# Mixing four chunks of attention logits with quarter-array products instead of four full-array products

## The chip, the cores and the metric

The kernel runs on one core of one Trainium2 chip. The metric is the device time of one execution in microseconds (us). The kernel before was timed three times: 578.25, 578.26 and 579.37 us, median 578.26 us.

## The reference, cut to what matters

Talking-heads attention over 8 batches, 12 heads, 448 positions and 64 dimensions, followed by a feed-forward layer:

```python
scores = scale * np.matmul(q, k.transpose(0, 1, 3, 2))          # per head
scores = np.einsum('bhij,hg->bgij', scores, w_pre)              # heads mixed before the softmax
attn = np.exp(scores - np.max(scores, axis=-1, keepdims=True))
attn = attn / (np.sum(attn, axis=-1, keepdims=True) + 1e-09)
attn = np.einsum('bhij,hg->bgij', attn, w_post)                 # heads mixed after the softmax
attn_out = np.matmul(attn, v)
x = attn_out.transpose(0, 2, 1, 3).reshape(8 * 448, 768)
h = np.maximum(x @ w_in, 0.0)                                   # 768 -> 2048
out = (h * h) @ w_out                                           # 2048 -> 768
```

## The kernel before

**Chunks.** The mixing of heads is a 12 by 12 matrix applied to the logits of one query position. The kernel handles ten query positions at a time: a *chunk* is 10 positions by 12 heads, so 120 partitions by 448 keys. A batch has 45 chunks, in four blocks: a short block of 6 (the last 64 positions), and three blocks of 13 chunks, of which the first of each (`cc == 0`) takes positions left over from two blocks and the other 12 are regular. There are 360 chunks in all.

**One chunk's way through the engines.** `score` (L681) makes the logits of one head for 128 query positions on TensorE. With 64 dimensions to contract, two heads use the two halves of the array's rows at the same time. VectorE (DVE) or ScalarE (ACT) copies each result from its PSUM bank to `snat` (L487 and L489 are the two branches of the helper `copy`, so all copies have these lines). `relayout` then issues a DMA on SP's queue, which gathers ten positions of all twelve heads from `snat` into one of eleven buffers `sch`. `chunk` then records, in this order:

- the mix on TensorE (L807): one product of the 120 x 128 weight `wmix` (ten copies of the 12 by 12 matrix on the diagonal) with `sch`, 448 columns into one PSUM bank;
- the minimum of each row on DVE (L818; the weights carry the sign and the scale, so the minimum stands for the maximum), and the exponential with its row sum on ACT (L821), which frees the bank;
- a reciprocal for two chunks at a time on DVE (L827), and on GpSimd (POOL) `wq` (L830), the second mixing matrix times the reciprocals;
- four products on TensorE that transpose and mix the attention weights (L837), and their copy to `atb` on DVE or ACT.

There are six buffers each of `es` (the exponentials) and `wq`. When a half batch is complete, `av` (L882) multiplies by `v`, two heads side by side in the two halves of the array's columns. Then units of the feed-forward layer follow: L941 is its first product, L955 or L959 the relu, L962 the square on POOL, L980 the second product, and L1004 the store. In batch 0, 14 chunks are made by another way (L813); the change leaves these alone.

**What sets the order.** Everything is recorded as an `Op` with a priority, dependencies and a guessed duration, and the class `Planner` simulates the engines once, at build time, and writes one fixed order for each engine. At run time each engine takes its list in that order and waits on semaphores. Feed-forward products have the lowest priority and fill what the attention leaves free. The planner hands out the eight PSUM banks; `MOST` bounds how many each kind of work may hold ("m" logits, "a" transposed weights, "f" feed-forward, "g" scores and `av`; "mix" all but "f"). It also knows a mode of the array for each product: `ROWS` for two row halves, `COLS` for two column halves, and it counts `TURN = 95` ns where the mode changes. `AHEAD` says how many chunks ahead of its use a gather is due. The products of `still` (L1191) are fillers without a result; the kernel has 44 of them in the early part of the run.

Of the kernel before, what the change touches and what calls it, by code (L numbers as in the profile page):

```python
# [23 lines left out]
NJ = 3  # L24
# [5 lines left out]
KC = CI * H  # L30
C0 = [0, 6, 19, 32]
# [9 lines left out]
NE = 6  # L41
NSCH = 11
AHEAD = 7.0
# [3 lines left out]
ROWS, COLS = 1, 2  # L47
# [5 lines left out]
STAY = {ROWS: 2, COLS: 6}  # L53
# [4 lines left out]
MOST = {"m": 3, "a": 2, "f": 2, "g": 6, "mix": 7}  # L58
# [245 lines left out]
def kernel(  # L304
# [30 lines left out]
    sch = many(NSCH, "sch", [KC, S], BF16)  # L335
    schl = sb.tile([KC, S], BF16, name="schl")
    es = many(NE, "es", [KC, S], BF16)
    mn = many(NE, "mn", [KC, 1], F32)
    sm = many(NE // 2, "sm", [KC, 2], F32)
    rc = many(NE // 2, "rc", [KC, 2], F32)  # L340
    wq = many(NE, "wq", [KC, H, CI], BF16)
# [49 lines left out]
    wpre_rep = sb.tile([KC, H], F32, name="wpre_rep")  # L391
    wpost_rep = sb.tile([KC, H], F32, name="wpost_rep")
    smask = sb.tile([KC, CI], F32, name="smask")
    wmix = many(3, "wmix", [KC, P], BF16)
    for t_ in wmix:
        nc.vector.memset(t_[:, KC:P], 0.0)
    wback = sb.tile([KC, H, CI], F32, name="wback")
    nmask = sb.tile([KC, CI], F32, name="nmask")
    perm = sb.tile([KC, KC], BF16, name="perm")

    own = sb.tile([KC, H], F32, name="own")
# [14 lines left out]
    def pick(to, of, mask):  # L416
        parts = hr[0][0:KC, 0:H * H].rearrange("p (g h) -> p g h", g=H)
        nc.vector.tensor_tensor(
            out=parts, in0=wall[0:KC, H * H * of:H * H * (of + 1)].rearrange("p (h g) -> p g h", g=H),
            in1=mask[:, :].unsqueeze(1).to_broadcast([KC, H, H]), op=ALU.mult,  # L420
        )
        nc.vector.tensor_reduce(out=to[:, :], in_=parts, axis=AX.X, op=ALU.add)

    def pick_near():
        nc.vector.tensor_reduce(
            out=own[:, :], in_=ident[0:KC, 0:KC].rearrange("p (s h) -> p h s", s=CI), axis=AX.X, op=ALU.add,
        )
        pick(wpre_rep, 0, own)
        pick(wpost_rep, 1, own)
# [23 lines left out]
    def near_masks():  # L453
        nc.vector.tensor_reduce(
            out=smask[:, :], in_=ident[0:KC, 0:KC].rearrange("p (s h) -> p s h", s=CI), axis=AX.X, op=ALU.add,
        )
        nc.vector.tensor_scalar(
            out=nmask[:, :], in0=smask[:, :], scalar1=-SCALE, scalar2=1.0, op0=ALU.mult, op1=ALU.mult,
        )
        nc.vector.tensor_copy(  # L460
            out=perm[:, :].rearrange("k (s x p) -> k s x p", s=CI, x=2),
            in_=ident[0:KC, 0:KC].rearrange("k (s p x) -> k s x p", s=CI, x=2),
        )

    def near_mix():
        for t_ in wmix[1:]:
            nc.vector.tensor_tensor(
                out=t_[:, 0:KC].rearrange("p (s h) -> p s h", s=CI),
                in0=wpre_rep[:, :].unsqueeze(1).to_broadcast([KC, CI, H]),
                in1=nmask[:, :].unsqueeze(2).to_broadcast([KC, CI, H]), op=ALU.mult,  # L470
            )

    def near_back():
        nc.gpsimd.tensor_tensor(
            out=wback[:, :, :], in0=wpost_rep[:, :].unsqueeze(2).to_broadcast([KC, H, CI]),
            in1=smask[:, :].unsqueeze(1).to_broadcast([KC, H, CI]), op=ALU.mult,
        )
# [237 lines left out]
    def relayout(b, c):  # L715
# [8 lines left out]
        if r == 2 and cc == 0:  # L724
            src_of[n] = schl
            here.append(move(n, pri, 780, deps + side.get(b - 1, []), schl[24:96, :], sn[120:126, :, :], lat))
            return
# [12 lines left out]
        else:  # L740
            parts = [(blk, 0, KC, sn[cc - 1:cc + CPR * (CI - 1):CPR, :, :])]
        for of, r0, r1, srcs in parts:
            ns = 860 if r1 - r0 > 90 else 590
            relay_of.setdefault(of, []).append(move(n, pri, ns, deps + old, src_of[n][r0:r1, :], srcs, lat))
        if r == 0 and cc == 5 and b > 0:
            here.append(move(
                place_of(b, C0[2]), pri + 0.5, 500, deps + side.get(b - 1, []),
                schl[0:24, :], sn[124:P, 0:NPAIR, :], lat,
# [17 lines left out]

    def chunk(b, c):
        n = place_of(b, c)
        r, cc = block_of(c)
        rows = 96 if c == C0[2 if b else NJ] else KC  # L770
        ns = rows // H
        far = is_direct(b, c)
        src = None if far else src_of[n]
        wm = wmix[0 if r == 0 else 2 if cc == 0 and r < NJ else 1]
        back = wback_far if far else wback
# [75 lines left out]
        m = m_op[n] = add(  # L851
# [13 lines left out]
        w = wq_op[n] = add("POOL", 370, n + 0.5, f_wq, [s_, at_op.get(n - NE)] + (backed_far if far else backed), lat=70)  # L865
# [147 lines left out]
    def pieces(pair, pos, part=None):  # L1013
        e0, e1 = (0, DMODEL) if part is None else part
        got = []
        for bb in range(2):
            row = (2 * pair + bb) * S
            for j, first in enumerate(PLACES[bb]):
# [9 lines left out]
                view = out[row:row + CPR * CI * NJ, :].rearrange("(s c r) e -> r c s e", c=CPR, r=NJ)  # L1028
# [24 lines left out]
    def w_turn(slot):  # L1053
        nc.tensor.matmul(
            slot[0:KC, 0:KC], lhsT=perm[:, :], rhs=wmix[1][:, 0:KC], start=True, stop=True,
        )

    def w_put():
        for t_, hi in ((wmix[0], KC), (wmix[2], 24)):
            nc.vector.tensor_copy(out=t_[0:hi, 0:KC], in_=slots["m", "w"][0:hi, 0:KC])  # L1060
# [6 lines left out]
    backed.append(add("POOL", 420, NEAR_AT, near_back, [fetched, masked]))  # L1067
# [78 lines left out]
    def next_batch(b):  # L1146
# [11 lines left out]
        for r in range(NJ + 1):  # L1158
            for p in groups(b, r):
                score(b, r, p)  # L1160
            for c in range(C0[r], (C0 + [NCHUNK])[r + 1]):
                relayout(b, c)
# [26 lines left out]
    def stand(slot, mode):  # L1189
        k_, m_ = P // 2 if mode == ROWS else P, P // 2 if mode == COLS else P  # L1190
# [41 lines left out]
```

## Time and profile before

| | |
|---|---|
| median of three runs | 578.26 us |
| profiled execution, its own time | 577.99 us |
| its span, first to last instruction | 576.2 us |
| granted TensorE clock, mean over the span | 0.999 |
| TensorE products (PE) busy | 565.1 us, 98% |
| VectorE (DVE) busy | 510.2 us, 89% |
| ScalarE (ACT) busy | 445.9 us, 77% |
| GpSimd (POOL) busy | 329.4 us, 57% |

In the page, busy time of an engine is the union of its instructions. A product's own duration holds its way through the array, so neighbours overlap: what one costs on a full engine is the distance between the starts of two neighbours, which the timeline shows. The profiled execution's time is 1.8 us more than its span.

### The profile page before, as it was taken

The page shows a single profiled execution, that of the slowest core. Times are in us where ns is not written, and L with a number is a line of the kernel's source. Part 1 is how long each engine was busy: PE and PEld are TensorE (multiplying, and loading weights), DVE is VectorE, ACT ScalarE, POOL GpSimd, SP SyncE. Part 2 cuts the span into 40 slices and gives each one's busy share as a digit, 9 for nine tenths or more (in the row PEclk, how much of TensorE's full clock was granted, in tenths as well). Part 3 has the DMA queues.
Part 4 walks back from the last instruction along what each step waited for, and adds up shares of the span by engine and source line. Part 5 has one row for each costly group of instructions (what it writes and reads, how often), then busy time and mean ns, then how long its engine had stood idle before and what let it go on. Part 6 is the DMA issues. An engine that isn't in the chain of part 4 may idle for free.

```text
span 576.2 us, 16829 instructions
## 1 busy us (share of the span) xinstructions
PE 565.1 (98%) x5830; PEld 407.5 (71%) x5830; DVE 510.2 (89%) x1124; ACT 445.9 (77%) x1185; POOL 329.4 (57%) x609
## 2 busy tenths in 40 slices
PE   8999999999999999999999999999999999999997
PEld 5668766786776767677667677777758676767784
DVE  7999998999999999989899988999799898989442
ACT  5798988878778887988888988888888888888100
POOL 8267445764575548646567357845767444735341
PEclk9999999999999999999999999999999999999999
DMA  9999849963898639963697638984497646322021
GB/s 135 211 182 224 158 116 208 163 151 87 132 202 156 159 100 184 173 151 111 137 181 148 164 104 144 188 152 139 109 205 158 147 121 117 124 81 75 1 56 55
DMA packets 131678, 80.79 MB, mean 140 GB/s; under 512 B 59286, under 2 KB 126600, under 8 KB 131592
## 3 DMA queue, kind: packets, MB, share of 16 engines
q1 hardware_dynamic: 84760, 56.88, 40.3%
q0 software_dynamic: 46784, 22.81, 30.8%
q8 instruction: 45, 0.74, 0.6%
q14 instruction: 41, 0.34, 0.2%
q10 hardware_dynamic: 48, 0.02, 0.0%
HBM read 45.61 MB, written 11.01 MB: 98 GB/s over the span
## 4 chain that ended last, share of the span: by engine, by line
PE 87%; DVE 6%; DMA 3%; ACT 2%; issue 1%; POOL 0%; DVEq 0%; ACTq 0%; POOLq 0%
PE bank L980 24%; PE bank L941 23%; PE bank L837 12%; PE bank L807 11%; PE bank L882 7%; PE bank L681 6%; DMA sch<-snat 3%; PE bank L813 2%; DVE mn L818 1%; DVE atb L487 1%; DVE snat L487 1%; PE bank L1191 1%; ACT es L821 1%; DVE qn L612 1%; ACT snat L489 0%
## 5 line engine op out<-in xcount | busy, mean ns | idle before, releaser
L821 ACT ACTIVATE es<-bank,mn 120x448 bf16<-120x448 f32 x360 | 228.5, 643 | 37.0 <-DVE mn L818 32.6
L818 DVE TENSOR_REDUCE mn<-bank 120x1 f32<-120x448 f32 x360 | 209.7, 611 | 1.2 <-PE bank L807 1.1
L830 POOL TENSOR_SCALAR wq<-wback,rc 120x120 bf16<-120x120 f32 (+1 forms) x346 | 123.0, 367 | 148.4 <-DVE rc L827 90.3
L980 PE MATMUL bank<-w,h 128*128 128x384 bf16 (+2 forms) x912 | 184.1, 323 | 0.0
L941 PE MATMUL bank<-xt,w 128*128 128x256 bf16 (+1 forms) x1632 | 164.7, 254 | 0.3 <-ACT hr L959 0.2
L962 POOL TENSOR_TENSOR h<-hr 128x512 bf16<-128x512 f32 x112 | 116.4, 1041 | 64.8 <-DVE hr L955 34.9
L941 PEld LDWEIGHTS <-w 128*128 128x128 bf16 x1632 | 136.1, 98 | 22.8 <-issue 2.4
L837 PEld LDWEIGHTS <-es 120*112 120x112 bf16 (+1 forms) x1440 | 110.9, 129 | 27.7 <-ACT es L821 3.7
L837 PE MATMUL bank<-wq,es 120*112 120x120 bf16 (+1 forms) x1440 | 120.8, 217 | 0.5 <-ACT es L821 0.2
L980 PEld LDWEIGHTS <-h 128*128 128x128 bf16 x912 | 83.7, 98 | 51.7 <-issue 5.2
L487 DVE CAST atb<-bank 112x480 bf16<-112x480 f32 (+3 forms) x184 | 112.9, 622 | 7.8 <-PE bank L837 4.9
L489 ACT CAST atb<-bank 112x480 bf16<-112x480 f32 (+3 forms) x199 | 103.8, 537 | 19.1 <-PE bank L837 18.3
L807 PE MATMUL bank<-sch,wmix 120*128 120x448 bf16 (+1 forms) x339 | 108.2, 354 | 2.6 <-DVE snat L487 2.0
L487 DVE CAST snat<-bank 128x448 bf16<-128x448 f32 x153 | 89.1, 612 | 4.8 <-PE bank L681 2.7
L489 ACT CAST snat<-bank 128x448 bf16<-128x448 f32 x165 | 81.8, 546 | 7.7 <-PE bank L681 7.2
L821 ACT ACTIVATION_READ_ACCUMULATOR es<-bank,mn 120x1 f32 x360 | 75.1, 209 | 0.0
L955 DVE TENSOR_SCALAR hr<-bank 128x512 f32<-128x512 f32 x75 | 51.6, 688 | 19.3 <-PE bank L941 16.9
L807 PEld LDWEIGHTS <-wmix 120*128 120x128 bf16 (+1 forms) x346 | 31.2, 97 | 23.7 <-issue 10.9
L882 PE MATMUL bank<-atb,vs 112*64 112x192 bf16 (+3 forms) x864 | 40.4, 250 | 0.1
L681 PE MATMUL bank<-kt,qz 64*128 64x448 bf16 x276 | 39.7, 354 | 0.5 <-DVE snat L487 0.2
L882 PEld LDWEIGHTS <-vs 112*64 112x64 bf16 x864 | 36.5, 110 | 3.9 <-issue 2.4
L487 DVE COPY osb<-bank 128x384 f32<-128x384 f32 (+2 forms) x42 | 22.8, 543 | 16.8 <-PE bank L980 16.2
(72 smaller groups left out, 316.7 us busy)
## 6 DMA issues: line engine op xcount, KB each, us to landing
sch<-snat SPq DMA_DIRECT2D x318, 105.0 KB
out_dram<-osb SPq DMA_DIRECT2D x22, 360.0 KB
vs<-in_v_dram POOLq DMA_DIRECT2D x16, 336.0 KB, 8.4
ks<-in_k_dram POOLq DMA_DIRECT2D x14, 336.0 KB, 8.2
qs<-in_q_dram POOLq DMA_DIRECT2D x14, 288.0 KB, 9.1
w<-in_moe_w_in_dram POOLq DMA_DIRECT2D x6, 512.0 KB, 13.5
w<-in_moe_w_out_dram POOLq DMA_DIRECT2D x4, 768.0 KB, 21.4
out_dram<-osb SPq DMA_DIRECT2D x8, 192.0 KB
```

The costliest lines, as they stand in the source:

```text
L487: nc.vector.tensor_copy(out=out_, in_=in_)
L489: nc.scalar.copy(out=out_, in_=in_)
L681: nc.tensor.matmul(slot[:, 0:S], lhsT=lhsT, rhs=kt[i][half, :, at_, :], start=True, stop=True)
L807: nc.tensor.matmul(slot[:, 0:S], lhsT=wm[0:rows, :], rhs=src[0:rows, :], start=True, stop=True,)
L818: nc.vector.tensor_reduce(out=mn[i][0:rows, :], in_=slots[mk][0:rows, 0:S], axis=AX.X, op=ALU.min)
L821: nc.scalar.activation(out=es[i][0:rows, 0:S], in_=slots[mk][0:rows, 0:S], func=ACT.Exp, scale=-1.0, bias=mn[i][0:rows, 0:1], accum_out=sm ...
L830: nc.gpsimd.tensor_scalar(out=wq[i][0:rows, :, 0:ns], in0=back[0:rows, :, 0:ns], scalar1=rc[i // 2][0:rows, i % 2:i % 2 + 1], scalar2=1.0, ...
L837: nc.tensor.matmul(slot[0:P_KEYS, jb * H * ns:(jb + 1) * H * ns], lhsT=es[i][0:rows, jb * P_KEYS:(jb + 1) * P_KEYS], rhs=wq[i][0:rows, :, ...
L882: nc.tensor.matmul(v_[64 * hh:64 * hh + 64, i, 0:x1 - x0], lhsT=vs[:, 2 * c2 + hh, jb, :], rhs=atb[half][:, jb, 2 * c2 + hh, x0:x1], start ...
L941: nc.tensor.matmul(slot[:, j * w:(j + 1) * w], lhsT=w1[c2][:, (f0 + j) * 128:(f0 + j + 1) * 128], rhs=xt[:, c2, a:z], start=(c2 == 0), sto ...
L962: nc.gpsimd.tensor_tensor(out=h2_[:, f0:f0 + nf, 0:w], in0=hr[gi % 2][:, :].rearrange("p (f c) -> p f c", f=nf), in1=hr[gi % 2][:, :].rear ...
L980: nc.tensor.matmul(slot[:, 0:c1 - c0], lhsT=h2_[:, ft, mt * 128:(mt + 1) * 128], rhs=w2[:, ft, c0:c1], start=(ft == 0), stop=(ft == FT - 1),)
```

## The change

From batch 1 on (`PAIR_FROM = 1`), the 12 regular chunks of each of the three long blocks are mixed in groups of four: 36 chunks in each of seven batches, 252 of the 360, in 63 groups. The weight is block diagonal, so positions 0 to 4 of a chunk never meet positions 5 to 9. With four empty partitions put ahead (`UP = 4`, so 124 partitions in place of 120), the first five positions lie in partitions 0 to 63 and the last five in 64 to 123. One chunk's mix is then two products with weights of 64 by 64 (or 60) at two row halves of the array; and two chunks, each with its two halves, give four products that use the four quarters of the array. A group of four chunks is eight such products, 448 columns each, into four banks. One bank receives the first halves of two chunks, the next bank their second halves, so what the following steps see as a chunk is made of five positions of each. The positions that are gathered (`relayout`), the second mixing matrix (`wback_two`, `smask_two`) and the rows to which the output goes (`pieces`) are arranged for that.

The four gathers of a group are recorded together, with due times closer together, and `AHEAD` goes from 7.0 to 8.1. Logits may hold seven banks instead of three, and attention work as a whole all eight instead of seven. Buffers of 120 partitions get 124; at the start, GpSimd clears partitions 0 to 3 of the twelve gather buffers and sets three small buffers to one, and VectorE does a few more small steps. The number of all other products, of gathers and of fillers is as before.

```diff
 KC = CI * H
+KR = KC + 4
-AHEAD = 7.0
+AHEAD = 8.1
-ROWS, COLS = 1, 2
+ROWS, COLS, BOTH = 1, 2, 3
+PAIR_FROM, PAIRS, PAIR_MORE = 1, 2, 60
+UP = 4
-STAY = {ROWS: 2, COLS: 6}
+STAY = {ROWS: 2, COLS: 6, BOTH: 2}
-MOST = {"m": 3, "a": 2, "f": 2, "g": 6, "mix": 7}
+MOST = {"m": 7, "a": 2, "f": 2, "g": 6, "mix": 8}
...
+    for t_ in sm:
+        nc.gpsimd.memset(t_[:, :], 1.0)
+    nc.vector.memset(perm[:, 0:UP], 0.0)
+    for t_ in sch + [schl]:
+        nc.gpsimd.memset(t_[0:UP, :], 0.0)
...
+    def two_mask():
+        nc.vector.tensor_reduce(
+            out=smask_two[:, :].rearrange("p (s e) -> p s e", e=2),
+            in_=ident[0:KR, UP:KR].rearrange("p (e s h) -> p s e h", e=2, h=H), axis=AX.X, op=ALU.add,
+        )
...
-            parts = [(blk, 0, KC, sn[cc - 1:cc + CPR * (CI - 1):CPR, :, :])]
+            o = cc - 1
+            if b >= PAIR_FROM:
+                o, pri = o // 2 + CPR // 2 * (o % 2), n - o % (2 * PAIRS) + 0.1 * (o % (2 * PAIRS)) - AHEAD
+            parts = [(blk, 0, KC, sn[o:o + 1 + CPR * (CI - 1):CPR, :, :])]
...
+    def mix_two(b, cs):
+        ns = [place_of(b, c) for c in cs]
+        keys = [("m", n) for n in ns]
+        srcs = [src_of[n] for n in ns]
+        w = wmix[1]
+
+        def mms(*got):
+            for i in range(0, len(got), 2):
+                for y in range(2):
+                    for x in range(2):
+                        k0, k1 = (64, KR) if x else (0, 64)
+                        o0, o1 = (64, KR) if y else (0, 64)
+                        c0 = (64 if y else 60) if x else (UP if y else 0)
+                        nc.tensor.matmul(
+                            got[i + x][o0:o1, 0:S], lhsT=w[k0:k1, c0:c0 + o1 - o0], rhs=srcs[i + y][k0:k1, :],
+                            start=True, stop=True,
+                        )
+
+        op = add(
+            "PE", 190 * len(cs) // 2 + PAIR_MORE, ns[0], keep(keys, mms),
+            [x for n in ns for x in relay[n]] + [at_op.get(ns[0] - NE), w_ready], lat=200, bank=keys, mode=BOTH,
+        )
+        for n in ns:
+            m_op[n] = op
...
     def chunk(b, c):
+        two = b >= PAIR_FROM and r > 0 and cc > 0
+        rows = H * ns + (0 if far else UP)
-        m = m_op[n] = add(
+        m = m_op[n] = m_op[n] if two else add(
...
-                view = out[row:row + CPR * CI * NJ, :].rearrange("(s c r) e -> r c s e", c=CPR, r=NJ)
+                view = out[row:row + CPR * CI * NJ, :].rearrange(
+                    "(s c r) e -> r c s e", c=CPR // 2 if 2 * pair + bb >= PAIR_FROM else CPR, r=NJ,
+                )
...
+                elif o % (2 * PAIRS) == 0:
+                    for c_ in range(c, c + 2 * PAIRS):
+                        relayout(b, c_)
+                    mix_two(b, range(c, c + 2 * PAIRS))
                 chunk(b, c)
```

## The prediction

> **What bounds the kernel now.** I read the page first: its busy times, slices and chain, then the groups of instructions.
>
> ```profile
> PE 565.1 (98%) x5830; PEld 407.5 (71%) x5830; DVE 510.2 (89%) x1124; ACT 445.9 (77%) x1185; POOL 329.4 (57%) x609
> ...
> PE   8999999999999999999999999999999999999997
> DVE  7999998999999999989899988999799898989442
> ...
> PE 87%; DVE 6%; DMA 3%; ACT 2%; issue 1%; POOL 0%; DVEq 0%; ACTq 0%; POOLq 0%
> ...
> L821 ACT ACTIVATE es<-bank,mn 120x448 bf16<-120x448 f32 x360 | 228.5, 643 | 37.0 <-DVE mn L818 32.6
> L818 DVE TENSOR_REDUCE mn<-bank 120x1 f32<-120x448 f32 x360 | 209.7, 611 | 1.2 <-PE bank L807 1.1
> ...
> L807 PE MATMUL bank<-sch,wmix 120*128 120x448 bf16 (+1 forms) x339 | 108.2, 354 | 2.6 <-DVE snat L487 2.0
> ...
> L681 PE MATMUL bank<-kt,qz 64*128 64x448 bf16 x276 | 39.7, 354 | 0.5 <-DVE snat L487 0.2
> ```
>
> TensorE is busy in every slice, the chain that ended last is 87% TensorE, and the mixes waited 2.6 us in all. So a TensorE nanosecond saved in the body of the run is worth nearly a nanosecond, as long as the second engine, DVE, lets it be. How near DVE is shows in busy time by stretches:
>
> ```profile
> 120.00:180.00 60.00, 58.87 (x550) 41.71 (x549) 58.35 (x120) 47.17 (x129) 38.76 (x69) 1.00 0.76 145
> ...
> 60.00:480.00 420.00, 416.51 (x4316) 299.45 (x4316) 391.49 (x840) 353.56 (x946) 251.80 (x475) 1.00 0.76 149
> ```
>
> The columns are PE, its weight loads, DVE, ACT and POOL. DVE is busy 391.5 of 420 us, and 97% in one stretch without starving TensorE. The price of a product is in TensorE's timeline:
>
> ```profile
> 305.13 0.58 PE L837 MATMUL bank<-wq,es 120*112 120x120 bf16 x8
> 305.56 0.35 PE L807 MATMUL bank<-sch,wmix 120*128 120x448 bf16 x1
> 305.75 1.48 PE L941 MATMUL bank<-xt,w 128*128 128x256 bf16 x12
> 307.15 0.55 PE L681 MATMUL bank<-kt,qz 64*128 64x448 bf16 x4
> 307.64 0.55 PE L807 MATMUL bank<-sch,wmix 120*128 120x448 bf16 x2
> 308.03 0.71 PE L941 MATMUL bank<-xt,w 128*128 128x256 bf16 x5
> ...
> 311.56 2.17 PE L882 MATMUL bank<-atb,vs 112*64 112x192 bf16 x48
> 313.66 0.42 PE L837 MATMUL bank<-wq,es 120*112 120x120 bf16 x4
> ```
>
> From start to start one mix takes 305.75 - 305.56 = 0.19 us, two take 0.39. Four score products, in row halves, take 307.64 - 307.15 = 0.49 us, not 4 x 0.19 = 0.76: two run at once, so there are two rounds, some 0.385 us, and the rest is the switch out of the row mode. The 12 products ahead of them take 1.40 us, against 1.31 where the chain shows twelve alone: 0.09 to switch in. Over all such neighbours in the trace the median is 94 ns in and 93 ns out, and the second round starts 196 ns after the first. Column halves also run two at once: 48 products of 192 columns take 2.10 us, 44 ns each.
>
> **The mixes themselves.** Out go 252 products at 0.19 us: 63 groups x 0.756 = 47.6 us. In come 504 quarter products. Four at a time they make two rounds, priced as the scores' two: 0.196 + 0.189 = 0.385 us a group, 24.3 us. The listing of instructions counts 202 changes of array mode before and 321 after: 119 x 0.094 = 11.2 us more. Sum on TensorE: -47.6 + 24.3 + 11.2 = **-12.1 us**. No row shows four quarters at once. The bounds come from the nearest rows: row halves and column halves each double, and together quadruple (the sum above); or only one doubling holds (rival two). I take the first, since column halves with the same 112 rows and row halves with the same 128 columns both overlap fully here. If the second round's weight load is not hidden, about one switch, 0.094 us a group, comes on top: 5.9 us. In both half modes the trace shows the next round's loads issued under the running round (15 ns after its start in the scores), so I take 0 and keep 5.9 for the range.
>
> **DVE and ACT.** Their work per chunk stays: cost goes by columns (448), not partitions (the 96-row form of L818 takes 607 ns, the 120-row form 611). In the listing DVE has 11 score copies more, 6 copies of `atb`, 3 relus and 6 output copies fewer, and a few small rows: within 3 us either way. What changes is cover. If 9.5 us of the gain falls in the 420 us above, DVE is busy 391.5 of 410.5, 95%: below the 97% that it held once, but with little left. To see what that costs I cut both listings into stretches of 15 chunks and priced each engine's rows start to start (DVE 0.53 us per minimum and score copy, 0.57 per copy of `atb`). Taking in each stretch the larger of the two engines, before gives 444.8 us where TensorE's rows alone sum to 440.0 (chunks 45 to 355), after 447.1 for 436.1: 6.2 us more lost where DVE is the fuller one. With stretches of 45 chunks it is 442.2 for 440.0 and 437.3 for 436.1, 1.0 us less lost. The buffers reach over some six chunks, so the short stretch is nearer, but not wholly: I take **+3.5 us**, bounds -1 and +6.
>
> **The end.** After the last product of `av` the profile has only feed-forward products:
>
> ```profile
> 536.83 2.74 PE bank L882 x48
> 539.57 1.42 PE bank L941 x12
> 540.99 10.40 PE bank L980 x64
> 551.39 10.48 PE bank L941 x96
> 561.87 10.45 PE bank L980 x80
> ```
>
> That is 144 at 163 ns and 108 at 109 ns, 35.2 us. The listing of after leaves 110 and 96, 28.4 us. It is not a second gain: 6.8 us of filler has moved into the attention part, which is why that part gets shorter by only some 5 us of the sum, and DVE, which works there, tighter by less than it might.
>
> **The start.** GpSimd clears twelve buffers of 4 x 448 and three small ones behind the `qt` loads, ahead of the loads of `vs` and `w1`. Its 128x128 memset took 0.22 us and its 128x1 0.10, so by columns one of these takes 0.2 to 0.5 us: 3 to 6 us in all. Its queue was idle 4.89 us ahead of the first `wq` at 19.82, so that is late by 0 to 1.5 us, with the first product of L837 queued on TensorE behind it; in the listing that now has one more chunk of L813 (six products, 1.1 us) ahead of it. The `w1` loads land later, but the first product that reads them was at 42.9 us. DVE has one more reduce (`two_mask`, about 0.27 us by the row of `smask`), on the chain before the first score copies. I take **+0.5 us**. The other edits cost nothing: gathers are as many (318 full ones), SP's order moves by a chunk, and a group's fourth gather may start when the mix two groups before is done.
>
> **Sum.** -12.1 + 3.5 + 0.5 = -8.1 us, on 577.99 gives 569.9; the profiled run is 0.3 us below the median, so I predict 570.2.
>
> **A rule that speaks against it.** The Trainium skill (TensorE: Matmul & The Clock Gate, on packing small matmuls) says that weight loads overlap running products only where the row group differs; by that, quarters one above the other in the same rows would wait for each other, as in rival two. The trace disagrees for column halves: products of L882, all on the same 112 rows, start 3 ns apart and average 44 ns. By the rule the time would be rival two's, by the row the forecast's.
>
> **Rivals.** *One: DVE takes over.* The same change, but DVE's full stretches cost 8 to 10 us, not 3.5: 575 to 577. For it: 95% in a fixed order. Against: ACT (354 of 420) takes copies, and 97% was held. Chance 0.14.
>
> *Two: quarters run only two at a time.* A group then is four steps, 3 x 0.196 + 0.282 + 0.094 = 0.964 us against 0.756: 63 x 0.208 = +13.1, about 591 us (more if the loads are bare). This is also the case in which the change does not do what it says. Chance 0.08.
>
> *Three, slower: a group waits for its last bank.* Its first product needs all four banks copied empty, and behind it on TensorE stand the products whose copies DVE and ACT wait for. In the listing the TensorE work between a bank's last product and the group has a median of 2.3 us and a tenth of the cases under 1.8. A copy needs 0.165 (a product's tail, 354 - 189 ns) + 0.61 = 0.78 us, and 0.53 more for each DVE instruction ahead of it. With one ahead (1.31) all 252 banks are covered; with three (2.4) more than half are not. If half of the groups wait 0.6 us, 19 us is lost, net about +10: 586. It decides from 0.13 us a group (8.1 / 63). Against it: before, banks came back with the same cover and the mixes waited 2.6 us. Chance 0.11.
>
> **Numbers.** Forecast (565 to 574) 0.62, rival one 0.14, no change 0.05, rivals two and three 0.19. Within 0.2% (1.2 us, about what a measurement of this kernel can tell) is "same". The low end is the sum with DVE's bound of -1 and the start at 0: 565. The upper end must leave out no more than the two slow rivals: 578.5.
>
> **What would show it.** Right: groups of eight products some 0.58 us from start to the next work, products 4 ns apart within a round; mode changes near 94 ns; DVE at 94 to 95% between 60 and 480 us; a tail of 28 us; TensorE's waits a few us larger. Wrong: 0.96 us a group (rival two), or waits on DVE or ACT ahead of the groups of over 0.13 us each (rival three), or many ahead of L837 and L681 (rival one).

## The result: slower by 1.1%

The changed kernel takes 585.87 us (median of five runs, 582.31 to 586.21) against 578.38 us for the kernel before on the same chip. The ratio is 1.0113, interval 1.0082 to 1.0143: slower, 15.7 us above the forecast of 570.2 and outside its range. The profiled execution took 586.01 us with a span of 584.2 us (before: 577.99 and 576.2), so the spans differ by 8.0 us. All medians here and below are of executions in the usual, fast state; one of number 8's four was slow and is left out.

The page of the changed kernel, in the same parts as before: busy times, slices, chain, groups of instructions. Line numbers have moved (L681 is now L698, L807 is L853, L813 is L859, L818 is L864, L821 is L867, L837 is L883, L882 is L928, L941 is L987, L980 is L1026, the branches L487 and L489 of `copy` are L504 and L506); L800 is the group of quarters.

```profile
PE 565.3 (97%) x6082; PEld 393.1 (67%) x6082; DVE 507.1 (87%) x1131; ACT 447.4 (77%) x1190; POOL 332.8 (57%) x618
...
PE   8999999979999999999999999999999999999996
...
DVE  7999999979998898999889999998999898998541
...
PE 84%; DVE 6%; ACT 4%; DMA 2%; issue 2%; POOL 1%; DVEq 0%; ACTq 0%; POOLq 0%; SPq 0%
...
L867 ACT ACTIVATE es<-bank,mn 124x448 bf16<-124x448 f32 (+1 forms) x360 | 228.3, 644 | 40.7 <-DVE mn L864 34.1
L864 DVE TENSOR_REDUCE mn<-bank 124x1 f32<-124x448 f32 (+1 forms) x360 | 206.4, 611 | 7.0 <-PE bank L800 5.3
...
L698 PE MATMUL bank<-kt,qz 64*128 64x448 bf16 x276 | 41.1, 354 | 1.4 <-ACT qz L506 0.7
...
L800 PE MATMUL bank<-sch,wmix 64*64 64x448 bf16 x504 | 36.2, 361 | 0.0
```

TensorE's busy time is what it was (565.3 against 565.1), although its work is less; its share of the chain is down from 87 to 84%, one slice (the ninth) shows a 7, and DVE, far from being fuller, is less busy and waits 7.0 us ahead of its minima. The groups L800 themselves waited 0.0 us. The same two stretches as before:

```profile
120.00:180.00 60.00, 59.01 (x593) 42.12 (x593) 53.85 (x115) 49.57 (x134) 37.98 (x66) 1.00 0.79 142
60.00:480.00 420.00, 409.78 (x4450) 281.67 (x4449) 381.65 (x829) 343.55 (x919) 244.62 (x457) 1.00 0.78 147
```

Between 60 and 480 us, every engine is less busy than before: TensorE 409.8 (416.5), DVE 381.7 (391.5), ACT 343.6 (353.6), POOL 244.6 (251.8). Over this stretch no engine has become the bound; they wait for each other. In places one is: from 208.0 to 218.4 us DVE was busy 10.1 of 10.4 us, TensorE 9.1. TensorE's timeline around one group:

```profile
111.31 0.49 PE L1026 MATMUL bank<-w,h 128*128 128x384 bf16 x2
111.64 0.37 PE L883 MATMUL bank<-wq,es 124*112 124x120 bf16 x4
111.95 0.57 PE L800 MATMUL bank<-sch,wmix 64*64 64x448 bf16 x8
112.45 0.50 PE L1026 MATMUL bank<-w,h 128*128 128x384 bf16 x2
```

Eight products take 0.50 us to the next work, the switch out included; four `wq` products ahead of them take 0.31 us, 0.10 more than the 0.21 of the same four ahead of a full product in experiment 1. One group costs 0.60 us against 0.756. Over all groups, product by product: four start at 0, 3, 7 and 10 ns, the second four 213 ns after the first, the next work 503 ns after the start, and the switch in is 93 ns. So the quarters do what they were meant to do.

The waits of TensorE, largest first (us in total, times, longest):

```profile
PE bank L698 <- ACT snat L506: 3.2, 2, 3.0
PE bank L883 <- ACT es L867: 2.1, 7, 0.7
PE bank L853 <- DMA sch<-snat: 1.7, 1, 1.7
...
PE bank L883 <- POOL wq L876: 0.8, 3, 0.4
```

This view counts a wait only where the array ran empty. A product that starts late while the one before is still on its way through (354 ns against 189 ns from start to start) shows nothing there. So I took an account from starts: every product costs the distance to the next start, and what a distance has over the usual one (189 ns for 448 columns and in proportion, 93 ns for a change of mode) is put down as a wait where it is above 60 ns.

| us of TensorE's time, start to start | before | after | difference |
|---|---|---|---|
| mixes (full; after: full 19.2 and quarters 31.9, with the switch out) | 67.8 | 51.1 | -16.7 |
| all other products, with the switches into groups and 1.1 us ahead of the first product | 491.2 | 500.5 | +9.3 |
| waits (62 before, 118 after; 1.7 us after are a slower clock, see below) | 13.1 | 27.2 | +14.1 |
| from the last product's start to the end | 4.1 | 5.4 | +1.3 |

These rows sum to 8.0 us, the spans' difference. The gain is there, 63 switches in at 0.093 take back 5.9 of it (the other 3.4 of that row are delays under 60 ns, which I did not follow), and the waits take more than the rest. A wait is for a PSUM bank where the last reader of the product's bank ended within 0.22 us before its start: such waits rose from 8.5 to 17.7 us, all others from 4.5 to 9.5. None of the waits stands ahead of a group. Most stand ahead of the full mixes (4.4 us), the two forms of scores (4.2 and 2.6), `still` (3.7) and the feed-forward's second product (1.7), and at the `wq` products (7.5). Between 60 and 480 us all eight banks were held at once for 8.6% of the time (5.4% before); a bank of logits is held for 3.6 us from its first write to its last read, against 3.06.

Some 1.7 us that the account puts down as waits, 1.3 of it at `av`, is none. In this profile the granted clock was 0.50 for 3.4 us, right behind a stretch (216.0 to 218.4 us) in which TensorE was busy for 1.5 of 2.4 us; the profile before has no such stretch in its body. Forty-eight `av` products took 4.10 us in it, and as many of the same size 2.81 elsewhere:

```profile
218.40:221.80 3.40, 3.40 (x31) 2.44 (x32) 2.85 (x8) 2.59 (x8) 2.14 (x5) 0.50 0.35 117
...
219.16 4.10 PE L928 MATMUL bank<-atb,vs 112*64 112x256 bf16 x48
...
152.31 2.81 PE L928 MATMUL bank<-atb,vs 112*64 112x256 bf16 x48
```

So the waits proper rose by some 12.4 us. This is not what made the kernel slower: the execution with a mean granted clock of 1.000 took 585.87 us, the median. Such stretches of half clock put about 1 us into the waits of numbers 2, 3, 4, 9, 13 and 16 below, 1.5 into those of 1 and 6, 2.0 to 2.6 into those of 7, 8, 12, 14 and 15, and nothing into those of 5, 10 and 11.

The ninth slice's 7 is one event. SP's queue just before it:

```profile
105.16 1.36 SPq L613 DMA_TRANSPOSE zt<-qt  x1
106.63 5.07 SPq L642 DMA_TRANSPOSE kt<-kn  x1
111.80 0.83 SPq L726 DMA_DIRECT2D sch<-snat  x1
112.73 1.89 SPq L648 DMA_TRANSPOSE qz<-qn  x1
```

The same transpose before the change:

```profile
107.76 1.50 SPq L625 DMA_TRANSPOSE kt<-kn  x1
```

The transpose that fills `kt` held the queue for 5.07 us, up to 5.0 of it by SP's list of waits for POOL's `wq`; the one before the change held it 1.50. Gathers behind it came late, `snat` was not free, and ACT stood still at its next copy:

```profile
116.54 0.24 ACT L867 ACTIVATION_READ_ACCUMULATOR es<-bank,mn 124x1 f32 x1
120.23 0.53 ACT L506 CAST snat<-bank 128x448 bf16<-128x448 f32 x1 [3.45 <-issue]
```

TensorE's next scores waited for the bank of that copy: the 3.0 us at the head of the waits, 3.2 us in the account. So 3.2 of the 14.1 us is a single place and 1.7 the clock; the rest is spread.

The end of the run, from the chain of waits:

```profile
550.38 2.74 PE bank L928 x48
553.12 4.98 PE bank L1026 x30
558.10 10.48 PE bank L987 x96
568.58 10.45 PE bank L1026 x80
```

After the last `av`, the products take 25.9 us (4.98 + 10.48 + 10.45) against 32.8 before. So 6.8 us of filler did move into the attention part.

### The profile page after: what moved, and what is told of

The parts are those of the page before. It is cut to its first block, busy times and chain, and to the rows that moved or that the text cites. A ratio compares the mean times of both kernels' runs of the same rounds, so it can differ in the third digit from the quotient of the medians.

```text
span 584.2 us, 17387 instructions
## 1 busy us (share of the span) xinstructions
PE 565.3 (97%) x6082; PEld 393.1 (67%) x6082; DVE 507.1 (87%) x1131; ACT 447.4 (77%) x1190; POOL 332.8 (57%) x618
## 4 chain that ended last, share of the span: by engine, by line
PE 84%; DVE 6%; ACT 4%; DMA 2%; issue 2%; POOL 1%; DVEq 0%; ACTq 0%; POOLq 0%; SPq 0%
PE bank L987 25%; PE bank L1026 24%; PE bank L883 13%; PE bank L928 6%; PE bank L698 5%; PE bank L800 5%; PE bank L853 3%; ACT es L867 3%; DVE mn L864 3%; DMA sch<-snat 2%; PE bank L1247 1%; DVE osb L842 1%; DVE snat L504 1%; DVE atb L504 1%; PE bank L566 1%
## 5 line engine op out<-in xcount | busy, mean ns | idle before, releaser
L867 ACT ACTIVATE es<-bank,mn 124x448 bf16<-124x448 f32 (+1 forms) x360 | 228.3, 644 | 40.7 <-DVE mn L864 34.1
L864 DVE TENSOR_REDUCE mn<-bank 124x1 f32<-124x448 f32 (+1 forms) x360 | 206.4, 611 | 7.0 <-PE bank L800 5.3
L1026 PE MATMUL bank<-w,h 128*128 128x384 bf16 (+2 forms) x912 | 176.5, 323 | 0.9 <-DVE snat L504 0.3
L987 PE MATMUL bank<-xt,w 128*128 128x256 bf16 (+1 forms) x1632 | 163.5, 254 | 0.3 <-ACT es L867 0.3
L987 PEld LDWEIGHTS <-w 128*128 128x128 bf16 x1632 | 132.8, 98 | 27.1 <-issue 13.5
L876 POOL TENSOR_SCALAR wq<-wback_two,rc 124x120 bf16<-124x120 f32 x252 | 89.8, 369 | 101.3 <-DVE rc L873 79.9
L883 PEld LDWEIGHTS <-es 124*112 124x112 bf16 (+2 forms) x1440 | 106.3, 129 | 38.1 <-issue 8.8
L506 ACT CAST atb<-bank 112x480 bf16<-112x480 f32 x197 | 105.6, 547 | 27.4 <-PE bank L883 26.7
L883 PE MATMUL bank<-wq,es 124*112 124x120 bf16 (+2 forms) x1440 | 120.1, 218 | 3.8 <-ACT es L867 2.1
L1026 PEld LDWEIGHTS <-h 128*128 128x128 bf16 x912 | 80.7, 98 | 61.0 <-issue 20.9
L504 DVE CAST atb<-bank 112x480 bf16<-112x480 f32 (+3 forms) x186 | 112.1, 610 | 8.7 <-PE bank L883 7.6
L504 DVE CAST snat<-bank 128x448 bf16<-128x448 f32 x164 | 95.6, 612 | 4.2 <-PE bank L698 2.3
L506 ACT CAST snat<-bank 128x448 bf16<-128x448 f32 x154 | 76.6, 549 | 13.0 <-PE bank L698 8.1
L867 ACT ACTIVATION_READ_ACCUMULATOR es<-bank,mn 124x1 f32 (+1 forms) x360 | 76.0, 211 | 0.0
L876 POOL TENSOR_SCALAR wq<-wback,rc 124x120 bf16<-124x120 f32 (+1 forms) x94 | 33.6, 365 | 55.1 <-DVE rc L873 37.3
L698 PE MATMUL bank<-kt,qz 64*128 64x448 bf16 x276 | 41.1, 354 | 1.4 <-ACT qz L506 0.7
L928 PE MATMUL bank<-atb,vs 112*64 112x192 bf16 (+3 forms) x864 | 41.7, 254 | 0.0
L928 PEld LDWEIGHTS <-vs 112*64 112x64 bf16 x864 | 37.4, 112 | 5.6 <-issue 4.9
L800 PE MATMUL bank<-sch,wmix 64*64 64x448 bf16 x504 | 36.2, 361 | 0.0
L873 DVE RECIPROCAL rc<-sm 124x2 f32<-124x2 f32 x180 | 27.6, 154 | 9.1 <-ACT es L867 8.0
```

The lines of the kernel that those rows point to most:

```text
L504: nc.vector.tensor_copy(out=out_, in_=in_)
L506: nc.scalar.copy(out=out_, in_=in_)
L698: nc.tensor.matmul(slot[:, 0:S], lhsT=lhsT, rhs=kt[i][half, :, at_, :], start=True, stop=True)
L800: nc.tensor.matmul(got[i + x][o0:o1, 0:S], lhsT=w[k0:k1, c0:c0 + o1 - o0], rhs=srcs[i + y][k0:k1, :], start=True, stop=True,)
L864: nc.vector.tensor_reduce(out=mn[i][0:rows, :], in_=slots[mk][0:rows, 0:S], axis=AX.X, op=ALU.min)
L867: nc.scalar.activation(out=es[i][0:rows, 0:S], in_=slots[mk][0:rows, 0:S], func=ACT.Exp, scale=-1.0, bias=mn[i][0:rows, 0:1], accum_out=sm ...
```

## The experiments

The theories at the outset were: the *side edits* (limits on banks, `AHEAD`) cost what was lost; the *groups* do, since four banks at once are taken and handed back in a lump; or *DVE* hands banks back too late. Each edit is against the changed kernel unless it says "before". Ratios, each with its 95% interval, are against the kernel before on the same chip; "waits" are those of the account above, in the profiled execution. Differences between two experiments are of medians, taken in part on different chips, on which the kernel before took 578.34 to 579.21 us: up to 0.9 us of such a difference can be the chip.

### What the groups bring and what the side edits cost

**1. Groups of four full products.** The order of all engines stays as in the changed kernel; each group is four 124 x 128 products.

```diff
-                        nc.tensor.matmul(
-                            got[i + x][o0:o1, 0:S], lhsT=w[k0:k1, c0:c0 + o1 - o0], rhs=srcs[i + y][k0:k1, :],
...
+            for slot, src in zip(got, srcs):
+                nc.tensor.matmul(slot[:, 0:S], lhsT=w[0:KR, :], rhs=src[0:KR, :], start=True, stop=True)
```

> The changed kernel with the same order on every engine; only the eight quarter products of each group are replaced by four full-array products, one per bank, so the heads of a chunk are mixed with the wrong partners and the output is other numbers. By the starts in the changed kernel's trace a group of quarters costs 0.503 us plus 0.094 for the switch ahead of it, 0.60 us; four full products 0.756. Theory 'banks' (TensorE waits because a group takes four of eight PSUM banks at once, and the feed-forward products that should fill find none): 63 x 0.16 = 10 us more TensorE work, of which part falls into the waits of today: 588 to 596 us. Theory 'quarters are dear' (the products or mode switches themselves cost what was lost): the same or less than the changed kernel, 578 to 586 us. Theory 'side edits' (limits, AHEAD, start): 594 to 596, nothing absorbed.

Measured: 590.01 us, ratio 1.0202 (1.0171 to 1.0232), waits 23.9 us. Its timeline at the same place:

```profile
111.82 0.37 PE L875 MATMUL bank<-wq,es 124*112 124x120 bf16 x4
112.03 0.92 PE L795 MATMUL bank<-sch,wmix 124*128 124x448 bf16 x4
112.79 0.49 PE L1018 MATMUL bank<-w,h 128*128 128x384 bf16 x2
```

Four full products take 0.76 us from start to start. With quarters the same order is 4.1 us faster. That shows that the quarters are not what makes the kernel slow. By the expectation, 590 spoke for the groups' banks and against the side edits; number 2 turns that round. But 63 x (0.756 - 0.597) = 10.0 us was taken off the products: in an order with this many waits, under half of a saved TensorE microsecond reaches the end.

**2. No groups, the new limits.** All batches are mixed one chunk at a time, as before; `AHEAD` and the limits stay new.

```diff
-PAIR_FROM, PAIRS, PAIR_MORE = 1, 2, 60
+PAIR_FROM, PAIRS, PAIR_MORE = 8, 2, 60
```

> The changed kernel with groups from batch 8 on, so none: every chunk is mixed by one full-array product as before, with the 124-partition layout, the start, AHEAD 8.1 and the new limits (seven banks for logits, eight for attention). 'Banks', in the form that the groups cause it: the waits go and the time is that of before plus what the start costs, 578 to 580 us. 'Side edits': it stays at 584 us or more, since the limits let attention take all eight banks with or without groups.

**3. No groups, the old limits.** What is left of the change is the layout of 124 partitions and the small steps at the start.

```diff
-AHEAD = 8.1
+AHEAD = 7.0
...
+PAIR_FROM, PAIRS, PAIR_MORE = 8, 2, 60
...
-MOST = {"m": 7, "a": 2, "f": 2, "g": 6, "mix": 8}
+MOST = {"m": 3, "a": 2, "f": 2, "g": 6, "mix": 7}
```

> As the run without groups, but AHEAD 7.0 and the old limits (three banks for logits, seven for attention): what is left is the 124-partition layout, the clears at the start on GpSimd and the extra rows on VectorE. If these cost what the prediction took, 578.5 to 579.5 us; if the start is the cause, 582 us or more.

Measured: number 2 took 589.30 us, ratio 1.0175 (1.0137 to 1.0212), waits 24.6; number 3 took 578.67 us, ratio 1.0003 (0.9982 to 1.0024), waits 13.7. These two kernels have the same products, and differ only in the limits and the order that follows from them. The stretch from 60 to 480 us of number 2:

```profile
60.00:480.00 420.00, 412.15 (x4166) 290.69 (x4167) 383.36 (x833) 348.72 (x934) 250.96 (x476) 1.00 0.76 146
```

and of number 3:

```profile
60.00:480.00 420.00, 416.20 (x4312) 299.42 (x4313) 393.01 (x846) 352.75 (x943) 251.19 (x473) 1.00 0.77 149
```

With the new limits TensorE loses 4 us, DVE 10 and ACT 4 in this stretch, without a single group in the program; in the account, waits of 24.6 against 13.7 us are the whole difference of 10.6 us in the medians. So the side edits cost by themselves more than the whole loss. By medians, in this order of steps: layout and start +0.3 (number 3), limits and `AHEAD` +10.6 (2 against 3), groups -3.4 (the changed kernel against 2). That makes +7.5. In another order of steps the parts would be other ones (numbers 7 and 15).

The waits of number 2 are no longer those of one line:

```profile
PE bank L853 <- DVE snat L504: 2.1, 4, 1.3
...
PE bank L853 <- DMA sch<-snat: 1.6, 3, 1.2
...
PE bank L883 <- POOL wq L876: 0.9, 3, 0.4
PE bank L883 <- ACT es L867: 0.8, 3, 0.3
```

Mixes wait for `snat` copies and gathers, `wq` products for POOL and ACT, none of them for long: the loss is spread over many handovers.

### Which of the side edits

**5, 6 and 11. One limit at a time, without groups.** All have `PAIR_FROM = 8`; number 5 gives attention the eighth bank, number 6 gives logits seven banks, number 11 has the new `AHEAD`.

```diff
# 5
+AHEAD = 7.0
+MOST = {"m": 3, "a": 2, "f": 2, "g": 6, "mix": 8}
# 6
+AHEAD = 7.0
+MOST = {"m": 7, "a": 2, "f": 2, "g": 6, "mix": 7}
# 11
 AHEAD = 8.1
+MOST = {"m": 3, "a": 2, "f": 2, "g": 6, "mix": 7}
```

> No groups, AHEAD 7.0, three banks for logits as before; the only limit changed is that attention work may hold all eight banks instead of seven, so that no bank is kept for the feed-forward products. Without groups the old limits gave 578.7 us and the new ones with AHEAD 8.1 589.3. Theory 'eighth bank': most of the 10.6 us comes back here, 584 to 589 us. Theory 'seven banks of logits' (mixes run too far ahead): 578 to 580. Theory 'any other order' (the order of before is a lucky one, and each change of a limit costs some us): 580 to 583, like the next run.

> No groups, AHEAD 7.0, attention seven banks as before; logits may hold seven of them instead of three. 'Eighth bank': 578 to 580 us. 'Seven banks of logits': 584 to 589. 'Any other order': 580 to 583.

> No groups, old limits, AHEAD 8.1: the third of the side edits by itself (the eighth bank alone gave 583.8 us, seven logit banks alone 580.4, none of the three 578.7, all three 589.3). If the three add up, 578.7 + 10.6 - 5.1 - 1.7 = 582.5 us; if the eighth bank and the early gathers only hurt together, 578.5 to 580.

Measured: number 5 took 583.84 us, ratio 1.0091 (1.0075 to 1.0108), number 6 580.40, ratio 1.0029 (1.0012 to 1.0045), number 11 586.45, ratio 1.0122 (1.0069 to 1.0175). Over number 3 that is +5.2, +1.7 and +7.8 us. The last is wide: its runs went from 581.74 to 589.53, and the profiled one was the lowest, so its trace says little about the median. The three sum to 14.7 where all together cost 10.6, so they do not simply add up, as the expectation of 582.5 us for number 11 had it. With the eighth bank for attention all eight banks are held 7.5% of the time (5.8 in number 3, 5.7 in number 6, 5.9 in number 11): that limit is the one that shows in the banks. Yet its waits rose by only 2.0 us (15.7 against 13.7), no more than number 6's do once the half clock is taken out; the profiled execution of number 5 also had 2.8 us outside its span where the others have 1.8, and 54 fillers in place of 44.

**12. How much a mere reordering moves.** In the kernel before, `AHEAD` goes the other way.

```diff
-AHEAD = 7.0
+AHEAD = 6.5
```

> The kernel before with AHEAD 6.5 instead of 7.0, nothing else: how much another order of the same instructions costs by itself. Theory 'any other order is worse': 580 to 583 us, in which case one or two us of each limit's price are of this kind. If the order matters little: 577.5 to 579.5.

Measured: 580.55 us, ratio 1.0031 (1.0014 to 1.0048), waits 15.8, of which 2.4 are half clock. An order that nothing else calls for costs about 2 us here (0.8 to 2.8 by the interval). So a difference of 2 us between two of these orders, number 6 for one, names no cause.

### Can the groups do without the side edits

**7 and 15. Groups without the eighth bank; groups with the old `AHEAD`.**

```diff
# 7
-MOST = {"m": 7, "a": 2, "f": 2, "g": 6, "mix": 8}
+MOST = {"m": 7, "a": 2, "f": 2, "g": 6, "mix": 7}
# 15
-AHEAD = 8.1
+AHEAD = 7.0
```

> The changed kernel, groups of four, AHEAD 8.1, but attention may hold seven banks only, so that one stays for the feed-forward products. 'Eighth bank' alone would give back up to 10 us: 576 to 580. 'Groups need the eighth bank' (a group must find four banks free at once among seven that scores, transposed weights and older logits also use): no gain or a loss, 586 to 594 us, with the waits ahead of attention products instead of feed-forward ones.

> The changed kernel with AHEAD 7.0, groups and new limits kept. Without groups and with the old limits AHEAD 8.1 cost 3 to 10 us. If early gathers are what costs, this run gives 578 to 581 us. If the banks are the cause and AHEAD is a choice that goes with the groups, 585 to 592.

Measured: number 7 took 592.27 us, ratio 1.0236 (1.0214 to 1.0257), waits 29.5; number 15 took 594.42, ratio 1.0276 (1.0255 to 1.0297), waits 32.8. Two of the edits that cost time without groups save time with them, 6.4 and 8.6 us. Number 7 came out as its second theory had it, number 15 above both of its ranges. In number 15 the groups themselves wait, which they do not in the changed kernel:

```profile
PE bank L800 <- DMA sch<-snat: 1.8, 2, 1.0
PE bank L800 <- ACT es L867: 1.0, 1, 1.0
```

Part of the gathers then come too late for their group. Number 7's waits are of another kind:

```profile
PE bank L883 <- POOL wq L876: 8.1, 10, 2.3
PE bank L853 <- DMA sch<-snat: 3.2, 1, 3.2
...
PE bank L698 <- ACT es L867: 1.1, 3, 0.6
```

What is late here is `wq`: ten waits, 8.1 us, where the changed kernel has three of 0.8 us in all. A likely reason is that groups which find no fourth free bank come later in the order; that was not followed. With groups of four, these two edits are worth keeping, and without groups the side edits cost more than the groups gain. The planner gives a group all its banks at once, so logits must be allowed four at the least; four to six of them, with the eighth bank, were not run.

**4. Groups of two chunks.** Two banks instead of four, with the limits nearly as before.

```diff
+AHEAD = 7.0
+PAIR_FROM, PAIRS, PAIR_MORE = 1, 1, 20
+MOST = {"m": 4, "a": 2, "f": 2, "g": 6, "mix": 7}
```

> Groups of two chunks: four quarter products, one round, two banks, 126 groups; limits of four banks for logits and seven for attention, AHEAD 7.0. By the trace of the changed kernel a lone round costs 0.29 us with the switch out and 0.094 in, 0.384, against 0.378 for two full products: no gain on TensorE unless two groups stand together. 'Banks': the waits go back to about those of before (13 us) and the time to 575 to 580 us. 'Quarters are dear': 252 mode changes more than before at 0.094 us in all, and the time over 588.

Measured: 580.71 us, ratio 1.0038 (1.0017 to 1.0058), waits 13.7. One such group in its timeline:

```profile
202.56 0.55 PE L698 MATMUL bank<-kt,qz 64*128 64x448 bf16 x4
203.04 0.38 PE L800 MATMUL bank<-sch,wmix 64*64 64x448 bf16 x4
203.35 0.42 PE L883 MATMUL bank<-wq,es 124*112 124x120 bf16 x4
```

Small groups keep the waits at the level of number 3, but one round has to pay for both switches. From start to next start it is 0.31 us with the switch out (median of the 112 groups that stand alone, 0.314), so 0.41 us with 0.094 for the switch in: more than the 0.384 of the expectation, and more than the 2 x 0.189 = 0.378 us of two full products. Time and waits fit 'banks' (580.71 is just above its range), but nothing is gained. That leaves little room between: the group must be large to pay for its switches, and small to need no other limits.

**8. Groups of four, small scores, one spare bank.** Scores take one bank at a time instead of two, and only a group may take the last bank.

```diff
-GROUP = 2
+GROUP = 1
...
-            return len(free) >= size and room[kind] >= size and (room["mix"] >= size or kind == "f")
+            spare = kind != "f" and not (kind == "m" and size > 2)
+            return len(free) >= size and room[kind] >= size and (room["mix"] >= size + spare or kind == "f")
```

`AHEAD` is 7.0 here.

> Groups of four as in the changed kernel, AHEAD 7.0, but only groups may take the eighth bank, and scores are made for one pair of heads at a time (two banks at once instead of four). If banks are what is short, TensorE's waits fall from 27 us to about 15; the smaller scores add some 60 rounds of their own with mode changes (about 0.1 us each in and out less those that stand together: 4 to 8 us). Sum on 585.9: -12 + 6, 578 to 582 us. If banks are not the cause, the waits stay and the added mode changes make it 588 us or more.

**16. Groups from batch 4 on.**

```diff
+PAIR_FROM, PAIRS, PAIR_MORE = 4, 2, 60
```

> The changed kernel with groups from batch 4 on: 36 groups instead of 63, limits and AHEAD as changed. The run without any groups gave 589.3 us and that with 63 gave 585.9. If each group saves alike, 589.3 - 3.4 x 36/63 = 587.4 us. If the loss sits in batches 1 to 3, where the feed-forward layer has just begun and has least to fill with, and groups are what makes it, 580 to 584.

Measured: number 8 took 589.50 us (median of three, 584.49 to 593.22), ratio 1.0180 (1.0112 to 1.0249), waits 23.9: the attempt to build a better version failed. By the expectation this speaks against a want of banks; but its old `AHEAD` alone costs much (number 15), so the run does not judge the spare bank. Number 16 took 584.27, ratio 1.0094 (1.0079 to 1.0110), waits 22.6: with the new limits in the whole run and groups in half of the batches, it lies within the changed kernel's scatter. That is below 587.4 us, what equal savings by each group would give, and just above the range for a loss that sits in batches 1 to 3.

### Is it the hand-back of the banks

**9 and 10. Half the minimum.** In both kernels DVE reduces half of the columns.

```diff
# 9 in the changed kernel, 10 in the kernel before
-            nc.vector.tensor_reduce(out=mn[i][0:rows, :], in_=slots[mk][0:rows, 0:S], axis=AX.X, op=ALU.min)
+            nc.vector.tensor_reduce(out=mn[i][0:rows, :], in_=slots[mk][0:rows, 0:S // 2], axis=AX.X, op=ALU.min)
```

> The changed kernel, same order everywhere, but the minimum (L864) reads 224 of the 448 columns, so it is taken over half of the keys. A minimum then costs VectorE about 0.30 us instead of 0.53, and the four banks of a group come back up to 0.9 us sooner. Theory 'late banks' (TensorE waits for banks and weights that DVE and ACT hand back too slowly): its waits of 27 us fall below 15 and the time to 570 to 576 us, at or below the kernel before with the same edit, since its TensorE work is 7 us less. Theory 'the order itself' (a transpose that holds SP's queue, gathers): less than 4 us gained, 582 us or more.

> The kernel before with the same edit (L818 reads 224 of 448 columns). Its waits are 13 us, half of them in the first 60 us, where the minimum matters little: 571 to 575 us under either theory. It is the yardstick for the run of the changed kernel with half the minimum.

Measured: number 9 took 581.50 us, ratio 1.0048 (1.0025 to 1.0071), waits 22.5; number 10 took 574.69, ratio 0.9926 (0.9905 to 0.9947), waits 9.7. The gains are alike, 4.4 and 3.7 us; number 9's lies between the ranges of its two theories. The stretch from 60 to 480 us in number 9, then in number 10:

```profile
60.00:480.00 420.00, 412.63 (x4476) 283.28 (x4475) 330.05 (x836) 346.89 (x928) 245.80 (x460) 1.00 0.79 148
...
60.00:480.00 420.00, 418.01 (x4347) 301.48 (x4346) 334.67 (x844) 355.51 (x950) 252.68 (x477) 1.00 0.74 150
```

In number 9 DVE is down to 330 of 420 us, 79%, and TensorE still loses 7.4 us there; in number 10, at the same load of DVE, it loses 2.0. A busy DVE is not what sets the changed kernel apart.

**13 and 14. Half the exponential.** In the changed kernel and in the kernel before, ACT takes the exponential of half of the columns; the other half of `es` holds ones.

```diff
# 13 in the changed kernel, 14 in the kernel before
+    for t_ in es:
+        nc.vector.memset(t_[:, S // 2:S], 1.0)
...
-                out=es[i][0:rows, 0:S], in_=slots[mk][0:rows, 0:S], func=ACT.Exp, scale=-1.0,
+                out=es[i][0:rows, 0:S // 2], in_=slots[mk][0:rows, 0:S // 2], func=ACT.Exp, scale=-1.0,
```

> The changed kernel, same order everywhere, but the exponential (L867) and its row sum take 224 of the 448 columns; the other half of each es buffer is set to one once at the start (six clears on VectorE in its idle time at 1.6 us). A logit bank then comes back about 0.19 us sooner, a group's last one about 0.7 us. In the traces TensorE's waits for a bank that an exponential had held are 6.5 us in the changed kernel and 1.1 in the kernel before. Theory 'banks held by logits': this run gains 6 to 10 us (576 to 580), more than the kernel before does with the same edit. Theory 'the order itself' (queues on SP and GpSimd): both gain alike, 3 to 4 us, 582 here.

> The kernel before with the same edit (L821). 'Banks held by logits': 575 to 577.5 us, a gain of 1 to 3. 'The order itself': 574 to 575, a gain like that of the changed kernel.

Measured: number 13 took 583.71 us, ratio 1.0087 (1.0061 to 1.0112), waits 25.6; number 14 took 578.83, ratio 0.9998 (0.9986 to 1.0010), waits 15.6. The exponential is the last reader of a bank of logits, and waits for a bank after it did fall, from 6.5 to 3.0 us; but waits for banks after other readers rose, those after the `atb` copies on DVE from 1.5 to 2.8 us and those after the `snat` copies from 6.6 to 7.2, and only 2.2 us was gained. In the kernel before, nothing was. Neither theory had that. No single hand-back carries the waits: shortened at one place, they come up at the next.

## Why the prediction was wrong, point by point

- **The mixes themselves (-12.1): right.** The account has -16.7 for the mixes with the switches out and +5.9 for those in, -10.8 together. The term was 1.3 us too good: a group takes 0.597 us, not 0.573, since the second round starts 213 ns after the first, not 196. (The sign, 0.58 us "from start to the next work", holds with the switch in counted; without it that distance was 0.50.) The mode changes were 93 ns, and as many as listed (321).
- **Loads under a running round: right, against the rule.** The second round's four weight loads were issued 27 to 35 ns after the first round's start, and four quarters ran at once. By the rule of the Trainium skill (TensorE: Matmul & The Clock Gate, on packing small matmuls), the quarters of the same rows would have had to wait for each other; this case's trace disagrees here too. Rival two is out.
- **DVE and ACT (+3.5): the cover was misjudged.** I forecast DVE at 94 to 95% between 60 and 480 us; it was at 90.9%. I took the fuller of two engines in each stretch as the price. Over the stretch the price was in neither of them, but in waits between them. Rival one is out as the main cause (numbers 9 and 10), though DVE is full in places.
- **The end (28.4 us): the shift right, the size not.** I forecast 35.2 - 28.4 = 6.8 us of filler moved; measured 32.8 - 25.9 = 6.8. Both tails were priced some 2.5 us too long, at the durations of larger products. As I held, it is no second gain.
- **The start (+0.5): right.** GpSimd's clearing took some 5 us of the 3 to 6 that I gave it, and number 3 puts the start and layout together at +0.3 (-1.0 to 1.4 by its interval).
- **"The other edits cost nothing": the step that failed.** I named the gathers and SP's order there, and never priced the two things that the diff says in one line each: `MOST` and `AHEAD`. They cost 10.6 us without any group (2 against 3), where the term was 0. SP's order, which I did name, cost 3.2 us at one place. Singly it is the eighth bank (+5.2) and `AHEAD` (+7.8, wide) more than the seven logits (+1.7, no more than a mere reordering).
- **Rival three (0.11, 586): the time and the resource, not the place.** It had the groups wait for their last bank. They waited 0.0 us; the planner gave them their banks in time, and other products waited: 9.2 us more for banks and 3.3 us more for other things, with 1.7 us of half clock beside them. Its own sum, 578.3 - 8.1 + 18.9, is 589 and not 586, so that 586 is near the measured time is luck. With the old `AHEAD` (number 15) groups do wait, 3.6 us in all. "TensorE's waits a few us larger" was 14.1, or 12.4 without the half clock. My argument against it, that before the change banks came back with the same cover and the mixes waited 2.6 us, was taken under limits that the change lifts.

What stays open: the planner rewrites the whole order for each limit, so the runs do not separate a shortage of banks from an order that is merely worse. The higher share of all eight banks held, with the eighth bank open to attention, speaks for the first, though number 7, with seven banks for attention, has 7.4% too; number 12's 2 us speak for part of the second. How many gather buffers (eleven) and buffers of `es` and `wq` (six) there are was changed in no run. With groups, the price of the side edits cannot be read at all, since groups without them are slower still. Which waits the `AHEAD` of 8.1 makes is not known, since its only profile was its lowest run. The transpose's 5.07 us on SP recurs in kernels with the same order (2.7 us of TensorE's time in number 9, 2.3 in number 1), and was not tested by an edit of its own. No kernel that does the whole work was faster than the one before.

## What to carry to other kernels

Where several engines are busy 75 to 98% and hand PSUM banks around, price every constant that feeds the order (limits on banks, due times) as an edit of its own, and run it alone before the new instruction. Here the products that need four banks at once showed no wait themselves; the limits that make room for them lengthened the waits of everything else, with groups or without (24.6 us in number 2, which has none). When a page shows all engines less busy than before, look for waits that are too short for the list of waits, by the distances between the starts of products.

## What was not expected of the hardware

- Four 64 x 64 products of 448 columns start within 10 ns and run together; a second round follows 213 ns after the first, against 196 ns for pairs of row halves and 189 ns for full products. Changing into or out of the quarters costs 93 ns, as for halves. On its own, one round of four with both switches (0.41 us) costs more than two full products (0.378 us).
- In the profile of the changed kernel the granted clock fell to 0.50 for 3.4 us in the middle of the run, and `av` products took 4.10 us in place of 2.81. Neither the list of waits nor the page's row of clock tenths shows it; the stretches and the mean clock (0.997 against 0.999) do.
- From the last product's start to the end of the span it was 5.3 to 5.7 us in every kernel with groups, and 4.1 us in all without. The difference lies behind the last copy to `osb`, in the last stores; the runs do not show more.
